# A decode kernel whose TensorE loop takes in its last round, and whose engines first visit the end of their programs

## The chip, the cores and the metric

The kernel runs on one core of one Trainium2 chip. The time is the device time in microseconds (us) of that core, and the value quoted is the median of several executions. The profile is of one execution: of the kernel before it is one more (664.23 us). Its span, from the first to the last instruction of the program, is 1.7 to 1.9 us shorter than the device time. The engines are TensorE (PE), VectorE (DVE), ScalarE (ACT), GpSimd (POOL) and SyncE (SP), which here only issues DMA transfers: all loads but that of x, and the output. SPq, PEq and DVEq are the parts of SyncE, TensorE and VectorE that issue (sequencers). PEld is TensorE loading weights.

## The reference, cut to what matters

One token passes through an attention block (32 query heads, 8 key/value heads, a cache of 65,536 positions of 128 numbers in bf16) and through a gated MLP (512 to 1,792 to 512), each with a layer norm and a residual sum.

```python
q = (layernorm(x) @ wq)                              # 512 -> 32 heads of 128
scores = einsum("bhqd,bhkd->bhqk", q, k) * 128**-0.5 # 4 query heads share one K head
o = einsum("bhqk,bhkd->bhqd", softmax(scores), v)
h = x + o @ wo
n = layernorm(h)
out = h + (sigmoid(n @ w_gate) * (n @ w_up)) @ w_down
```

The two caches are 8 x 65,536 x 128 x 2 bytes = 134 MB each. The weights add about 14 MB.

## The kernel before

The kernel loads each head's K and V in four blocks of 4 MB (so 32 K blocks and 32 V blocks, K0 to K31 and V0 to V31) into a ring of four slots. VectorE transposes a K block, TensorE forms its scores, the softmax of a head follows its fourth block, and the products with V follow one head later. Near the end the kernel loads wo, the last V blocks, then w_gate, w_up and w_down.

The kernel records all operations first and then writes them out for each engine. TensorE's operations of rounds 0 to 7 (one round for each head) form one loop. The parts A0 to A3 are the scores of a K block, the parts B0 to B3 the products of the V block of the head before, which round 0 skips. The ninth round (only B parts, for head 7, with the output projection in between) is written out after the loop:

```python
P.rounds = {"pe": (0, HKV), "dve": (1, HKV)}
...
with eng.Fori(lo, hi) as i:
    for p in order:                       # A0 B0 A1 B1 A2 B2 A3 B3
        with ExitStack() as cond:
            if lo not in parts[e][p]:
                cond.enter_context(eng.If_ne(i.val[eng.engine], lo))
            for o, w in zip(parts[e][p][hi - 1], plan[p]):
                put(e, eng, o, w)
...
for o in tail:                            # round 8, projection, MLP
    put(e, eng, o, waits_of(e, o, seen, off, False))
```

The loads are issued by SyncE in a fixed order. Each waits until the load that had its slot four loads ago has been used:

```python
order = [("wq", 0)]
order += [("K", b) for b in range(NR)]
for b in range(NR, NB):
    order += [("K", b), ("V", b - NR)]
order += [("V", NB - 4), ("V", NB - 3), ("V", NB - 2), ("V", NB - 1), ("wg", 0), ("wu", 0), ("wd", 0)]
for i, ld in enumerate(order):
    slot_of[ld] = i % NSLOT
    prev[ld] = order[i - NSLOT] if i >= NSLOT else None
```

## Time and profile before

| what | value |
|---|---|
| time, median of 3 (later of 4) runs | 664.56 us (664.51) |
| bytes moved by DMA | 282.33 MB |
| DMA busy, mean of 16 engines | 99.3% of the span |
| TensorE busy, VectorE busy | 64%, 53% |
| last piece of w_down landed | 659.50 us after the start of the span |
| end of the span | 662.6 us |

These are lines of the profile page of the kernel before: the busy time of TensorE and the other engines; the busy tenths of the DMA engines and what they moved, in 40 equal slices; the DMA queues with packets, megabytes and share; and the chain that ended last, by engine.

```profile
PE 424.0 (64%) x2385; PEld 80.5 (12%) x1617; DVE 350.6 (53%) x443; ACT 38.1 (6%) x106; POOL 5.4 (1%) x12
...
DMA  9999999999999999999999999999999999999997
GB/s 380 439 420 435 437 423 437 433 423 441 429 425 441 425 431 439 423 436 433 425 437 433 425 439 431 425 437 431 427 439 425 433 435 425 437 433 410 426 427 292
...
q1 hardware_dynamic: 11560, 282.33, 99.3%
q8 instruction: 4, 0.07, 0.0%
q14 instruction: 2, 0.02, 0.0%
...
DMA 71%; DVE 22%; PE 6%; issue 1%; SPq 0%; ACT 0%
```

DMA is at 9 tenths in 39 of 40 slices, no compute engine is near that, and the chain of waits is 71% DMA. The kernel is a stream of loads, and all else fits beside it. Two lines deserve a look: those of the queues that the page calls "instruction". I read their packets as the engines' own programs on their way in, and call them fetches; the run of GpSimd with a long program bears that out, where 2,048 more instructions bring sixteen packets of 8 KB. They move little (six packets, 80 KB), but each lasts 0.31 to 1.08 us, and the landing marks below show what that does to the stream.

The start and the end of the timeline before (start, duration, engine, source line, operation, destination and source, count; in brackets the idle time before it and what ended it):

```profile
0.74 0.40 SPq L293 DMA_DIRECT2D ring<-in_A_wq_dram  x1
...
2.39 0.29 PE L375 MATMUL PS<-ident,x_row 1*128 1x1 bf16 x4 [2.39 <-DMA x_row<-in_A_x_dram]
...
13.17 9.74 PE L394 MATMUL PS<-ring,xz 128*8 128x512 bf16 x32 [7.44 <-DMA ring<-in_A_wq_dram]
```

```profile
630.20 0.33 SPq L297 DMA_DIRECT2D ring<-in_B_w_up_dram  x1
...
652.27 1.20 PE L640 MATMUL PS<-identf,hT 128*1 128x32 f32 x32
...
655.17 0.93 PE L632 MATMUL PS<-ring,hc 128*1 128x448 bf16 x16 [1.70 <-DMA ring<-in_B_w_up_dram]
...
658.91 1.02 PE L656 MATMUL PS<-ring,hhT 128*1 128x128 bf16 x28 [0.20 <-DMA ring<-in_B_w_down_dram]
...
659.98 0.29 DVE L660 CAST y_sb<-PS 128x128 bf16<-128x128 f32 x1 [2.24 <-PE PS L656]
660.30 0.66 SPq L661 DMA_DIRECT2D out_dram<-y_sb  x1
```

The end of the chain of waits before (start, duration, what):

```profile
640.55 18.31 DMA ring<-in_B_w_down_dram
...
658.91 1.05 PE PS L656 x25
...
659.98 0.29 DVE y_sb L660
```

The first product with wq starts at 13.17 us, when wq has landed. In the tail, the products with w_up start at 655.17, when w_up has landed, and the last ones with w_down at 658.91. From there only 3.7 us are left. (The trace counts each f32 matmul of L640 twice: its 32 are 16 in the program.)

**Landing marks.** One more reading is needed, and no view of the page gives it. The trace keeps 16 landing marks for every block, as many as the page counts DMA engines, and I read each mark as one engine that is done with its share. It fits this reading that after the first fetch just one of the 16 marks of K2 is late: it is 1.56 us behind the median, the next one 0.36. So for each transfer I can read when the median engine and the last engine were done. I call the difference the lag. The packet records of the trace, which give start, duration, size and queue of each DMA packet, show when the fetches ran. For the kernel before, in us from the start of the span:

```text
instruction packets inside the span: 16 KB at 36.6, 57.0, 623.3, 649.9 (1.02 to 1.08 us each)
                                      8 KB at 54.7, 297.6 (0.31 to 0.33 us each)
transfer          median engine   last engine   lag
K1                    32.10          32.46      0.36
K2                    41.82          43.38      1.56    (fetch at 36.6 lies before this)
K31                  585.80         587.36      1.56
w_down, piece 3      657.86         659.50      1.64
```

### The profile page before, as it was taken

How to read it: one execution, taken by the hardware profiler on the slowest of the kernel's cores; microseconds unless marked ns; L12 is line 12 of the kernel's file. 1: busy time of each engine (PE TensorE's matmuls, PEld its weight loads, DVE VectorE, ACT ScalarE, POOL GpSimd, SP SyncE). 2: the span in 40 equal slices, each digit the busy share in tenths (PEclk: the TensorE clock that was granted, in tenths of full speed). 3: DMA queues.
4: the chain of work that ended last, by engine and by line, in shares of the span. 5: the costliest groups of instructions: out<-in, count | busy, mean ns of one | idle time of the engine just before them, and what ended most of it. 6: DMA issues, size and time to landing. Idle time of an engine off the chain costs nothing.

```text
span 662.6 us, 4910 instructions
## 1 busy us (share of the span) xinstructions
PE 424.0 (64%) x2385; PEld 80.5 (12%) x1617; DVE 350.6 (53%) x443; ACT 38.1 (6%) x106; POOL 5.4 (1%) x12
## 2 busy tenths in 40 slices
PE   2787487548676575576665576765856667556744
PEld 1100010011010110011100111001100111001222
DVE  3598855556337654347555463466643565553002
ACT  0200200020000200020000200002000200002000
POOL 2000000000000000000000000000000000000000
PEclk9799687678877677776866688766878867766877
DMA  9999999999999999999999999999999999999997
GB/s 380 439 420 435 437 423 437 433 423 441 429 425 441 425 431 439 423 436 433 425 437 433 425 439 431 425 437 431 427 439 425 433 435 425 437 433 410 426 427 292
DMA packets 11568, 282.42 MB, mean 426 GB/s; under 512 B 1193, under 2 KB 2218, under 8 KB 2602
## 3 DMA queue, kind: packets, MB, share of 16 engines
q1 hardware_dynamic: 11560, 282.33, 99.3%
q8 instruction: 4, 0.07, 0.0%
q14 instruction: 2, 0.02, 0.0%
q10 hardware_dynamic: 2, 0.00, 0.0%
HBM read 282.33 MB, written 0.00 MB: 426 GB/s over the span
## 4 chain that ended last, share of the span: by engine, by line
DMA 71%; DVE 22%; PE 6%; issue 1%; SPq 0%; ACT 0%
DMA ring<-in_A_k_cache_dram 62%; DVE ktw L439 20%; DMA ring<-in_A_v_cache_dram 4%; DMA ring<-in_B_w_down_dram 3%; PE PS L452 2%; DMA ring<-in_A_wq_dram 2%; PE PS L394 1%; PE PS L529 1%; DVE M_sb L444 1%; PE PS L451 1%; SPq L313 0%; DVE PT_sb L501 0%; PE PS L656 0%; PE PS L478 0%; PE PS L485 0%
## 5 line engine op out<-in xcount | busy, mean ns | idle before, releaser
L439 DVE STREAM_TRANSPOSE ktw<-ring 128x1024 f32<-128x1024 f32 x256 | 291.8, 1207 | 166.3 <-DMA ring<-in_A_k_cache_dram 165.3
L452 PE MATMUL PS<-ktw 128*128 128x512 bf16 x768 | 271.4, 452 | 54.2 <-DVE ktw L439 54.2
L451 PE MATMUL PS<-ktw 128*128 128x512 bf16 x256 | 119.0, 465 | 116.7 <-DVE ktw L439 114.9
L529 PE MATMUL PS<-ring,PT_sb 128*16 128x512 bf16 x1024 | 75.1, 444 | 12.8 <-DMA ring<-in_A_v_cache_dram 11.6
L451 PEld LDWEIGHTS PS<-ktw 128*128 128x128 bf16 x256 | 27.7, 108 | 432.8 <-issue 274.4
L501 DVE STREAM_TRANSPOSE PT_sb<-P_sb 128x512 bf16<-128x512 bf16 x32 | 20.2, 684 | 37.4 <-PE PS L539 36.0
L529 PEld LDWEIGHTS PS<-ring,PT_sb 128*16 128x16 bf16 x1024 | 30.6, 116 | 56.5 <-issue 30.0
L444 DVE TENSOR_REDUCE M_sb<-PS 128x1 f32<-128x512 f32 x32 | 19.9, 684 | 25.6 <-PE PS L451 25.6
L487 ACT ACTIVATE negmax<-PS 128x1 f32<-128x1 f32 x8 | 1.4, 171 | 545.8 <-PE PS L485 545.8
L491 ACT ACTIVATE P_sb<-PS,negmax 128x512 bf16<-128x512 f32 x32 | 21.5, 685 | 0.3
L508 DVE TENSOR_REDUCE lsum<-PS 128x1 f32<-128x4 f32 x8 | 1.3, 162 | 29.8 <-PE PS L506 29.8
L394 PE MATMUL PS<-ring,xz 128*8 128x512 bf16 x32 | 9.7, 478 | 7.4 <-DMA ring<-in_A_wq_dram 7.4
L354 DVE COPY hT<-PS 128x4 f32<-128x4 f32 x2 | 1.3, 629 | 24.9 <-PE PS L566 24.9
L478 PE MATMUL PS<-identf,gm 128*1 128x128 f32 x16 | 3.3, 292 | 17.0 <-DVE gm L476 17.0
L536 ACT ACTIVATE po_sb<-PS,rl 128x512 bf16<-128x512 f32 x8 | 5.7, 708 | 39.7 <-PE PS L529 39.7
L539 PE MATMUL PS<-sel_bf,po_sb 128*128 128x4 bf16 x32 | 2.1, 169 | 8.0 <-ACT po_sb L536 8.0
L485 PE MATMUL PS<-one_f,gmrep 1*128 1x1 f32 x16 | 4.0, 317 | 5.0 <-DVE gmrep L482 5.0
L491 ACT ACTIVATION_READ_ACCUMULATOR P_sb<-PS,negmax 128x1 f32 x32 | 6.5, 203 | 0.0
L369 POOL TENSOR_TENSOR rstd<-ve,nhalf 128x1 f32<-128x1 f32 x2 | 1.1, 553 | 645.7 <-DVE ve L367 645.7
L577 PE MATMUL PS<-ktw,O 128*1 128x512 bf16 x28 | 6.2, 379 | 0.0
L394 PEld LDWEIGHTS PS<-ring,xz 128*8 128x8 bf16 x32 | 3.2, 102 | 13.5 <-issue 11.3
L480 DVE TENSOR_REDUCE gmj<-PS 1x4 f32<-1x128 f32 x8 | 2.2, 278 | 4.1 <-PE PS L478 4.1
(85 smaller groups left out, 68.8 us busy)
## 6 DMA issues: line engine op xcount, KB each, us to landing
ring<-in_A_k_cache_dram SPq DMA_DIRECT2D x32, 4096.0 KB, 29.6
ring<-in_A_v_cache_dram SPq DMA_DIRECT2D x31, 4096.0 KB, 30.4
ring<-in_A_wq_dram SPq DMA_DIRECT2D x1, 4096.0 KB, 12.3
ring<-in_A_v_cache_dram SPq DMA_DIRECT2D x1, 3072.0 KB, 32.3
ktw<-in_A_wo_dram SPq DMA_DIRECT2D x1, 2048.0 KB, 9.6
ktw<-in_A_wo_dram SPq DMA_DIRECT2D x2, 1024.0 KB, 13.0
ring<-in_B_w_gate_dram SPq DMA_DIRECT2D x1, 1792.0 KB, 35.1
ring<-in_B_w_up_dram SPq DMA_DIRECT2D x1, 1792.0 KB, 24.9
```

Source lines behind the costliest of these rows:

```text
L394: op("pe", lambda e, kt=kt, n=n, last=last: e.matmul(ps(1, 0, 512, 0, 8), lhsT=xz[:, kt * 15 + 7 - n: kt * 15 + 15 - n], rhs=wq_v[:, kt, n ...
L439: op("dve", lambda e, d=dst, sr=src: e.transpose(d, sr), deps, f"T{b}.{c}", to="T")
L444: op("dve", lambda e, u=u: e.tensor_reduce(M_sb[:, u % 4:u % 4 + 1], ps(u % NS, 0, 512), AX.X, ALU.max), [f"S{b}.{NC - NR + k}"], f"mx{u}" ...
L451: return e.matmul(out, lhsT=lhsT, rhs=rhs, start=start, stop=stop)
L452: return e.add_instruction(mybir.InstMatmult(name=nc.get_next_instruction_name(), engine=mybir.EngineType.PE, ins=[e.lower_ap(rhs), e.lowe ...
L478: op("pe", lambda e: e.matmul(ps(MISC, 0, 128, 0, 1), lhsT=gm[:, :], rhs=identf[:, :], start=True, stop=True), [f"gm{h}"], f"gmT{h}", to="Q")
L485: op("pe", lambda e: e.matmul(ps(MISC, 128, 129), lhsT=gmrep[0:1, :], rhs=one_f[0:1, 0:1], start=True, stop=True), [f"gmrep{h}"], f"neg{h}")
L491: op("act", lambda e, b=b: e.activation(P_sb[:, (b % 4) * 512:(b % 4 + 1) * 512], ps(b % NS, 0, 512), AF.Exp, bias=negmax[:, k:k + 1], sca ...
L501: op("dve", lambda e, b=b: e.transpose(PT_sb[:, (b % 4) * 512:(b % 4 + 1) * 512], P_sb[:, (b % 4) * 512:(b % 4 + 1) * 512]), [f"E{b}", f"o ...
L529: op("pe", lambda e, lhsT=lhsT, tq=tq, t0=t0, c=c: e.matmul(ps(PO, 0, 512, 32 * tq, 32 * tq + 16), lhsT=lhsT, rhs=ring[:, s * SLOT + t0 * ...
L536: op("act", lambda e: e.activation(po_sb[:, :], ps(PO, 0, 512), AF.Copy, scale=rl[:, :]), [f"PV{NR * h + NR - 1}", f"rl{h}"], f"po{h}", to ...
L577: op("pe", lambda e, r=r, src=src, n=n, end=end: e.matmul(ps(YB, 0, D, 0, 1), lhsT=src[:, r:r + 1], rhs=ktw[:, r * D:(r + 1) * D], start=( ...
```

## The change

The change is meant to make the instruction fetches fewer and earlier. TensorE's ninth round moves into the loop: B parts run in rounds 1 to 8, A parts in rounds 0 to 7, and the projection (L) and the column step (C) only in round 8. The program becomes shorter by the second copy of the B parts. TensorE, VectorE and ScalarE run a loop of two passes around their whole programs. The first pass only branches to its end and back, under a branch hint for the back edge, which is meant to have the end of the program fetched before it is needed. For the loop to fit the last round, the last V blocks alternate between two slots, and the MLP weights get the two other slots, so that they wait for nothing in the tail. Some small operations of the tail are merged.

```diff
+                        if runs == [hi - 1]:
+                            cond.enter_context(eng.If_eq(reg, hi - 1))
+                        else:
+                            if runs[0] != lo:
+                                cond.enter_context(eng.If_ne(reg, lo))
+                            if runs[-1] != hi - 1:
+                                cond.enter_context(eng.If_lt(reg, runs[-1] + 1))
 ...
+        def twice(e, eng):
+            if self.ops[e][0]["dma"]:
+                put(e, eng, self.ops[e][0], [])
+                self.ops[e] = self.ops[e][1:]
+            with self.nc.Fori(0, 2, engines=OrderedEngineSet([eng.engine]), hint_back_edge=True) as z:
+                with eng.If_ne(z.val[eng.engine], 0):
+                    run(e, eng)
 ...
-            deco(lambda eng, e=e: run(e, eng))
+            deco((lambda eng, e=e: twice(e, eng)) if e in ("pe", "dve", "act") else (lambda eng, e=e: run(e, eng)))
 ...
+            if ld[0] == "V" and ld[1] >= NB - NR:
+                slot_of[ld] = slot_of["V", ld[1] - 2]
+                prev[ld] = ("V", ld[1] - 2)
+            elif ld[0][0] == "w" and i:
+                slot_of[ld] = 3 if ld[0] == "wd" else 1
+                prev[ld] = ("K", NB - 1 if ld[0] == "wd" else NB - 2)
 ...
-        P.rounds = {"pe": (0, HKV), "dve": (1, HKV)}
+        P.rounds = {"pe": (0, HKV + 1), "dve": (1, HKV)}
+        P.order = {"pe": ["A0", "B0", "L", "A1", "B1", "A2", "B2", "A3", "X", "C", "B3"],
+                   "dve": ["A0", "B0", "A1", "A2", "A3", "A4"]}
 ... (w_up in two pieces; 16 residual matmuls replaced by one of a spread copy of h; x added on VectorE)
```

More of the change, by code (lines that the diff above doesn't have):

```diff
@@ L4 @@
 from concourse import mybir
+from concourse.ordered_engine_set import OrderedEngineSet
 bf16 = mybir.dt.bfloat16
@@ L44, in __init__ @@
         self.rounds = {}
+        self.order = {}
         self.part = {}
@@ L143, in run @@
                     seq.append(o["part"])
-            order = [p for p, r in seq if r == hi - 1]
+            order = self.order[e]
             assert seq == [(p, r) for r in range(lo, hi) for p in order if r in parts[e][p]]
@@ L147, in run @@
                 s2 = {}
-                w = [waits_of(e, o, s2, off, True) for o in parts[e][p][r]]
+                w = [waits_of(e, o, s2, off, len(parts[e][p]) > 1) for o in parts[e][p][r]]
                 assert plan.setdefault(p, w) == w, (p, r)
@@ L155, in run @@
                         off[k] = off.get(k, 0) + n
-            regs = {}
             with eng.Fori(lo, hi) as i:
                 for p in order:
+                    runs = sorted(parts[e][p])
+                    reg = i.val[eng.engine]
                     with ExitStack() as cond:
-                        if lo not in parts[e][p]:
-                            cond.enter_context(eng.If_ne(i.val[eng.engine], lo))
-                        for o, w in zip(parts[e][p][hi - 1], plan[p]):
+                        if runs == [hi - 1]:
+                            cond.enter_context(eng.If_eq(reg, hi - 1))
+                        else:
+                            assert runs == list(range(runs[0], runs[-1] + 1)) and runs[0] - lo < 2
+                            if runs[0] != lo:
+                                cond.enter_context(eng.If_ne(reg, lo))
+                            if runs[-1] != hi - 1:
+                                cond.enter_context(eng.If_lt(reg, runs[-1] + 1))
+                        for o, w in zip(parts[e][p][runs[-1]], plan[p]):
                             put(e, eng, o, w)
@@ L204, in bass_sequential_preLN__gqa_block_cached__glu_gated_glu__decode_kernel @@
         yr = sb("yr", [1, 512], fp32)
+        gsel = sb("gsel", [128, 128], fp32)
+        hz = sb("hz", [128, 128], fp32)
         scr = sb("scr", [1, 64], fp32)
@@ L275, in bass_sequential_preLN__gqa_block_cached__glu_gated_glu__decode_kernel @@
         for i, ld in enumerate(order):
-            slot_of[ld] = i % NSLOT
-            prev[ld] = order[i - NSLOT] if i >= NSLOT else None
+            if ld[0] == "V" and ld[1] >= NB - NR:
[4 more added lines that the diff above has]
+                prev[ld] = ("K", NB - 1 if ld[0] == "wd" else NB - 2)
+            else:
+                slot_of[ld] = i % NSLOT
+                prev[ld] = order[i - NSLOT] if i >= NSLOT else None
         def freed(ld):
@@ L286, in bass_sequential_preLN__gqa_block_cached__glu_gated_glu__decode_kernel @@
         V_SPLIT = [(0, 6), (6, 8)]
+        W_SPLIT = {"wg": [(0, 4)], "wu": [(0, 3), (3, 4)]}
+        W_AT = {"wg": 0, "wu": 4 * FF}
         for ld in order:
@@ L296, in bass_sequential_preLN__gqa_block_cached__glu_gated_glu__decode_kernel @@
                 w = B_w_gate if k == "wg" else B_w_up
-                dma("sp", lambda e, d=dst, w=w: e.dma_start(d[:, 0:4 * FF].rearrange("p (k n) -> p k n", k=4),
-                    w.rearrange("(p k) n -> p k n", p=128)), f"r{s}", deps, k)
+                dst, src = dst[:, W_AT[k]:W_AT[k] + 4 * FF], w.rearrange("(p k) n -> p (k n)", p=128)
+                for i, (k0, k1) in enumerate(W_SPLIT[k]):
+                    dma("sp", lambda e, d=dst, w=src, a=k0 * FF, z=k1 * FF: e.dma_start(d[:, a:z], w[:, a:z]),
+                        f"{k}{i}", deps if i == 0 else (), f"{k}.{i}")
             elif k == "wd":
@@ L310, in bass_sequential_preLN__gqa_block_cached__glu_gated_glu__decode_kernel @@
                         dma("sp", lambda e, d=dst, sr=src, a=c0 * CH, z=c1 * CH: e.dma_start(d[:, a:z], sr[:, a:z]),
-                            f"vl{i}", deps if i == 0 else (), f"V{b}.{i}")
+                            "v0" if i else "vl", deps if i == 0 else (), f"V{b}.{i}")
                 else:
-                    dma("sp", lambda e, d=dst, sr=src: e.dma_start(d, sr), f"v{s}" if k == "V" and b < NB - NR else f"k{s}" if k == "K" and b >= NR else f"r{s}",
+                    dma("sp", lambda e, d=dst, sr=src: e.dma_start(d, sr), f"v{s}" if k == "V" else f"k{s}" if k == "K" and b >= NR else f"r{s}",
                         deps, f"{k}{b}")
@@ L348, in bass_sequential_preLN__gqa_block_cached__glu_gated_glu__decode_kernel @@
         op("dve", lambda e: e.tensor_copy(sel_bf[:, :], sel_f[:, :]), ["self"], "sel")
+        op("dve", lambda e: e.memset(gsel[:, :], 0.0), (), "gs0")
+        op("dve", lambda e: e.tensor_reduce(bass.AP(tensor=gsel, offset=0, ap=[[128, 128], [32, 4]]),
+                                            identf[:, :].rearrange("p (s j) -> p s j", s=4), AX.X, ALU.add), ["gs0", "identf"], "gsel")
         def ln_stats(i, src_dep, bank, c0):
@@ L378, in bass_sequential_preLN__gqa_block_cached__glu_gated_glu__decode_kernel @@
         op("pe", lambda e: e.matmul(ps(PO, 0, 512), lhsT=zrow[0:1, 0:128], rhs=zrow[0:1, :], start=True, stop=True),
-           ["zrow", "identf", "lsel", "onef", "sel"])
-        op("pe", lambda e: e.matmul(ps(5, 0, 128), lhsT=zrow[0:1, 0:128], rhs=zrow[0:1, 0:128], start=True, stop=True))
+           ["zrow", "identf", "lsel", "onef", "sel", "gsel"])
         ln_stats(0, ("xTp", (MISC, 0, 4)), 0, 0)
@@ L506, in denominators @@
             op("pe", lambda e: e.matmul(ps(MISC, 132, 136), lhsT=lsel[:, :], rhs=L_sb[:, :], start=True, stop=True),
-               [f"PT{NB - 1}"] if h == HKV - 1 else (), f"l{h}", to="Q")
+               [f"PT{NR * h + NR - 1}"], f"l{h}", to="Q")
             op("dve", lambda e: e.tensor_reduce(lsum[:, :], ps(MISC, 132, 136), AX.X, ALU.add), [f"l{h}"], f"ls{h}", to="D")
@@ L517, in pv @@
                     deps = []
-                    if b == NB - 1:
-                        for i, (c0, c1) in enumerate(V_SPLIT):
-                            if c == c0 and tq == 0:
-                                deps.append(f"V{b}.{i}")
-                    elif c == 0 and tq == 0:
-                        deps.append(f"V{b}")
+                    if tq == 0 and c == (V_SPLIT[1][0] if r == NR - 1 else 0):
+                        deps.append(f"V{b}" if b < NB - 1 else f"V{b}.1")
                     if c == 0 and tq == 0:
@@ L579, in project7 @@
                     skip_group_check=True), deps, "yr" if end else None)
-            op("dve", lambda e: e.tensor_copy(yr[:, :], ps(YB, 0, D, 0, 1)), ["yr"], "yrs")
+            op("dve", lambda e: e.tensor_tensor(yr[:, :], ps(YB, 0, D, 0, 1), x_row[:, :], ALU.add), ["yr"], "yrs")
         def columns():
@@ L587, in columns @@
                                                               stop=False, skip_group_check=True), ["yrs"] if nt == 0 else ())
-            op("pe", lambda e: e.matmul(ps(YT, 0, 4), lhsT=ident[:, :], rhs=xT[:, :], start=False, stop=False,
-                                        skip_group_check=True), ["xT"], "yx")
-        P.rounds = {"pe": (0, HKV), "dve": (1, HKV)}
+        P.rounds = {"pe": (0, HKV + 1), "dve": (1, HKV)}
+        P.order = {"pe": ["A0", "B0", "L", "A1", "B1", "A2", "B2", "A3", "X", "C", "B3"],
+                   "dve": ["A0", "B0", "A1", "A2", "A3", "A4"]}
         P.loop_sems = {"T": ("pe", "A3", NR * NC), "g": ("pe", "A3", 2), "W": ("pe", "A3", 1), "PT": ("pe", "B3", 1),
@@ L596, in bass_sequential_preLN__gqa_block_cached__glu_gated_glu__decode_kernel @@
         for i in range(HKV + 1):
+            loop = 0 < i < HKV
             for r in range(NR):
-                b, v = NR * i + r, NR * (i - 1) + r
-                P.part = {"pe": (f"A{r}", i), "dve": (f"A{r}", i) if i else None} if i < HKV else {}
+                P.part = {"pe": (f"A{r}", i), "dve": (f"A{r}", i) if loop else None}
                 if i < HKV:
-                    dve_block(b)
-                    pe_scores(b)
+                    dve_block(NR * i + r)
+                    pe_scores(NR * i + r)
                     if r == NR - 1:
                         softmax(i)
-                P.part = {"pe": (f"B{r}", i), "dve": (f"B{r}", i)} if i < HKV else {}
                 if i:
+                    v = NR * (i - 1) + r
+                    if r == NR - 1 and i < HKV:
+                        P.part = {"pe": ("X", i)}
+                        op("pe", lambda e: None, [f"V{v}"])
+                    elif r == NR - 1:
+                        P.part = {"pe": ("C", i)}
+                        columns()
+                        op("pe", lambda e: None, [f"V{v}.0"])
+                    P.part = {"pe": (f"B{r}", i), "dve": (f"B{r}", i) if loop else None}
                     if r == 0:
@@ L612, in bass_sequential_preLN__gqa_block_cached__glu_gated_glu__decode_kernel @@
                     if v == NB - 4:
+                        P.part = {"pe": ("L", i)}
                         project7()
-                    if v == NB - 2:
-                        columns()
-            P.part = {"dve": ("A4", i) if i else None}
+            P.part = {"dve": ("A4", i) if loop else None}
             if i < HKV:
@@ L625, in bass_sequential_preLN__gqa_block_cached__glu_gated_glu__decode_kernel @@
                                                    op0=ALU.mult, op1=ALU.add), ["tot.1"], "hc")
+        op("dve", lambda e: e.tensor_tensor(hz[:, :].rearrange("p (j k) -> p j k", k=4),
+                                            bass.AP(tensor=sel_f, offset=0, ap=[[32, 128], [1, 32], [0, 4]]),
+                                            bass.AP(tensor=hT[1], offset=0, ap=[[4, 128], [0, 32], [1, 4]]), ALU.mult),
+           ["hT.1", "self"], "hz")
         ln_rstd(1, STB, 0, 4.0)
@@ L628, in bass_sequential_preLN__gqa_block_cached__glu_gated_glu__decode_kernel @@
         for i, (nm, bank) in enumerate((("wg", GB), ("wu", UB))):
-            wv = slot_ap(slot_of[(nm, 0)])[:, 0:4 * FF].rearrange("p (k n) -> p k n", k=4)
+            at = slot_of[(nm, 0)] * SLOT + W_AT[nm]
             for kt in range(4):
                 for c in range(4):
-                    op("pe", lambda e, wv=wv, kt=kt, c=c, bank=bank: e.matmul(
-                        ps(bank, 0, FG, 32 * c, 32 * c + 1), lhsT=hc[:, kt:kt + 1], rhs=wv[:, kt, c * FG:(c + 1) * FG],
+                    dep = [f"{nm}.{j}" for j, (k0, _) in enumerate(W_SPLIT[nm]) if k0 == kt and c == 0]
+                    op("pe", lambda e, at=at, kt=kt, c=c, bank=bank: e.matmul(
+                        ps(bank, 0, FG, 32 * c, 32 * c + 1), lhsT=hc[:, kt:kt + 1],
+                        rhs=ring[:, at + kt * FF + c * FG: at + kt * FF + (c + 1) * FG],
                         start=(kt == 0), stop=(kt == 3), tile_position=(0, 32 * c)),
-                       ["hc", nm] if kt == 0 and c == 0 else (), f"gu{i}" if kt == 3 and c == 3 else None)
+                       ["hc"] * (kt == 0 and c == 0) + dep, f"gu{i}" if kt == 3 and c == 3 else None)
             if i == 0:
-                for g in range(4):
-                    for kt in range(4):
-                        dst = psap(YB, kt, [[4, 32]], 32 * g, 1)
-                        op("pe", lambda e, g=g, kt=kt, dst=dst: e.matmul(
-                            dst, lhsT=hT[1][:, kt:kt + 1], rhs=identf[:, 32 * g:32 * g + 32],
-                            start=(kt == 0), stop=False, tile_position=(0, 32 * g), skip_group_check=True),
-                           ["hT.1"] if g == 0 and kt == 0 else ())
+                op("pe", lambda e: e.matmul(ps(YB, 0, 128), lhsT=gsel[:, :], rhs=hz[:, :], start=True, stop=False, skip_group_check=True),
+                   ["hz"])
         op("act", lambda e: e.activation(sg[:, :], ps(GB, 0, FG), AF.Tanh, scale=rstd[1][:, 0:1]), ["gu0", "rstd.1"], "sg")
```

## The prediction

> **What bounds the kernel now.** The DMA stream. In the page's slices DMA is at 9 tenths in 39 of 40; its queue part gives 282.33 MB on one queue, 99.3% of 16 engines. The chain of waits is 71% DMA and ends in w_down landing at 658.87 us, then TensorE (1.05), the VectorE copy (0.29), the output DMA, end 662.6. TensorE is busy 64%, VectorE 53%. By the SyncE timeline, cache blocks are issued about 30 us before they land: nothing starves the queue. In the tail (timeline) TensorE is done with w_gate at 652.5 and waits for w_up until 655.17: 2.6 us to spare.
>
> **A small loss that the change aims at.** [...] its packet records have 16 KB instruction packets (TensorE's, I take it) at 36.6, 57.0, 623.3 and 649.9 us, about 1.04 us each, and 8 KB ones at 54.7 and 297.6. Each holds one DMA engine. In the 16 landing marks of each transfer the last engine is 0.36 us behind the median at 32 us, 1.56 at 43 (after the first fetch), and 1.64 at the last w_down piece (median 657.86, last 659.50). So fetches cost about 1.3 us at the end, as the largest lag of any engine, not as a sum.
>
> **What the change does.**
> - TensorE's last round goes into the loop: 631 matmuls in the program become 481, with weight loads about 1,255 instructions become 945: one block fewer.
> - TensorE, VectorE, ScalarE jump to the end first: last blocks are fetched[...] not at 297, 623, 650. This delays their start[...], hidden: the query matmul waits for wq until 13.17, its input is ready at 7.5.
> - About ten more branches per TensorE round: hidden; skipping a part in round 0 before shows no gap at 36.7.
> - The last V blocks share two slots; the MLP weights get slots freed by K30 and K31. V31 would be issued when V29's products end (630.2), 6.4 us before V30 lands (636.6): no starvation. Bytes and order stay.
> - 16 residual products become one (about 1 us of TensorE near 653, where it waits for DMA anyway), x is added on VectorE, w_up comes in two pieces: its last product starts 0.6 us earlier, then waits for w_down all the same.
>
> **On the critical path**: only the lag of the slowest DMA engine. I expect the fetches at 297, 623 and 650 us to go. But near 37 us TensorE still runs towards a middle block that the jump does not touch, so one fetch probably stays and leaves one engine 1.5 us behind to the end: gain about 0.2 us. If that one goes too, the gain is 1.2; if two fetches at the start meet on one engine, a loss of about 1.
>
> **Predicted**: 664.1 us, range 662.9 to 665.3. Faster by over 2%: 0.01; within: 0.98; slower: 0.01.
>
> **What would show it.** No instruction packets between 60 us and the end. V blocks still landing 9.7 us apart. Median engine's last landing near 657.9; last engine 1.2 to 1.6 behind. Chain still ends w_down, TensorE, copy, output.
>
> **What would make it wrong.** The two-slot ring starving the queue (a gap before V30 or V31, several us)[...]; the middle block fetched at the start too (663.2).

A "block" of a program is what one instruction packet carries. Its sum starts from the 664.56 us of the kernel before and has one term on the critical path, the lag: 0.2 us less (1.2 less if the fetch near 37 us goes too, about 1 more if two fetches meet on one engine). It came to 664.1 us; that is 0.26 below 664.56 - 0.2, and the text does not itemise the rest. The "one block fewer": the run with no jump shows it, with three 16 KB packets in place of four.

## The result and the profile after

| | before | after |
|---|---|---|
| median of 4 runs | 664.51 us (664.40 to 664.81) | 664.69 us (664.43 to 664.86) |
| ratio, 95% interval | | 1.0002 (0.9984 to 1.0019) |

The ratio is the mean time of the changed kernel's runs over that of the kernel before in the same rounds, so it is not quite the ratio of the medians. The time is the same; even the sign of the difference is open.

The same lines of the page after:

```profile
PE 426.3 (64%) x2353; PEld 79.6 (12%) x1585; DVE 351.1 (53%) x446; ACT 38.6 (6%) x106; POOL 5.4 (1%) x12
...
DMA  9999999999999999999999999999999999999996
GB/s 379 439 425 429 439 425 433 439 419 439 439 417 437 441 419 437 433 427 437 433 427 437 431 427 439 425 433 439 423 433 441 419 435 439 421 437 404 436 421 285
...
q1 hardware_dynamic: 11704, 282.33, 99.3%
q8 instruction: 3, 0.05, 0.0%
...
q14 instruction: 1, 0.00, 0.0%
...
DMA 66%; DVE 22%; PE 10%; issue 1%; SPq 0%; ACT 0%; DVEq 0%
```

The stream looks the same. The 16 KB instruction packets (queue q8) are three in place of four; of the 8 KB ones (q14) the line still lists one small packet, and the packet records show no 8 KB one before the end of the span. The same places of the timeline and of the chain:

```profile
0.74 0.39 SPq L322 DMA_DIRECT2D ring<-in_A_wq_dram  x1
...
8.44 0.26 PE L409 MATMUL PS<-ident,x_row 1*128 1x1 bf16 x4 [8.44 <-issue]
...
14.55 9.72 PE L427 MATMUL PS<-ring,xz 128*8 128x512 bf16 x32 [4.62 <-DMA ring<-in_A_wq_dram]
```

```profile
630.71 0.80 SPq L341 DMA_DIRECT2D ring<-in_A_v_cache_dram  x2
...
653.35 0.80 PE L678 MATMUL PS<-hz,gsel 128*128 128x128 f32 x2
...
659.17 1.01 PE L692 MATMUL PS<-ring,hhT 128*1 128x128 bf16 x28 [0.55 <-DMA ring<-in_B_w_down_dram]
...
660.23 0.29 DVE L696 CAST y_sb<-PS 128x128 bf16<-128x128 f32 x1 [2.62 <-PE PS L692]
660.55 0.65 SPq L697 DMA_DIRECT2D out_dram<-y_sb  x1
```

```profile
633.46 25.66 DMA ring<-in_B_w_down_dram
...
659.17 1.04 PE PS L692 x23
660.23 0.29 DVE y_sb L696
```

TensorE begins at 8.44 us, not at 2.39: its trip to the end of the program cost 6 us. It did not matter, because the products with wq waited for wq anyway. But they start at 14.55 us, not 13.17, and that is because wq itself lands later (14.41 us, against 13.03 before). The landing marks show why:

```text
after: instruction packets of 16 KB inside the span at 5.3, 36.9, 47.6; of 8 KB: none
transfer          median engine   last engine   lag    next two engines
wq                    12.71          14.41      1.71   0.36, 0.17
K2                    41.83          43.71      1.88   1.73, 0.17
K3                    51.53          53.44      1.90   1.73, 1.70
w_down, piece 3      658.07          659.75      1.69   1.52, 1.51
```

Each fetch beside the stream puts one DMA engine 1.7 to 1.9 us behind the median one, and that engine stays behind for the remaining 600 us. (The marks don't name their engine; that it is the same one is read from lags that hardly change from one block to the next.) Three fetches lie on three engines here. TensorE goes on only when the last engine has landed: the last products with w_down start at 659.17 us, after the last engine's 659.12 for the second piece, not after the median's 657.43. So the end of the stream is where it was: the lag was 1.71 us after the one fetch at 5.3 us and is 1.69 at the end, after three; before the change it was 1.64, after four and with one of them as late as 650 us.

The packet records show what a lag is made of. The fetch at 36.93 us lasts 1.05 us. The stream's next packet of 32 KB starts as it ends and takes 1.68 us, where 1.21 to 1.23 is usual. The 1.05 and the 0.47 on top make 1.5 us. Between 12 and 600 us just two of the 7,755 stream packets of that size are longer than 1.23 us, and both follow an instruction packet; before the change four are, and so do they.

One thing stays unexplained: from wo on, a fourth engine is 1.5 us behind, with no instruction packet near. It doesn't set the end, since others are further behind. V blocks still land 9.7 us apart (V29 to V30: 627.22 to 636.93), so the two slots of the tail do not starve the queue.

### The profile page after: what moved, and what is told of

It reads as the page before. It is cut to its first block, busy times and chain, and to the rows that moved or that the text cites. A ratio compares the mean times of both kernels' runs of the same rounds, so it can differ in the third digit from the quotient of the medians.

```text
span 663.0 us, 4962 instructions
## 1 busy us (share of the span) xinstructions
PE 426.3 (64%) x2353; PEld 79.6 (12%) x1585; DVE 351.1 (53%) x446; ACT 38.6 (6%) x106; POOL 5.4 (1%) x12
## 4 chain that ended last, share of the span: by engine, by line
DMA 66%; DVE 22%; PE 10%; issue 1%; SPq 0%; ACT 0%; DVEq 0%
DMA ring<-in_A_k_cache_dram 57%; DVE ktw L472 20%; PE PS L485 4%; DMA ring<-in_B_w_down_dram 4%; DMA ring<-in_A_v_cache_dram 3%; DMA ring<-in_A_wq_dram 2%; PE PS L558 2%; PE PS L484 2%; PE PS L427 1%; DVE M_sb L477 1%; DVE PT_sb L534 1%; PE PS L518 0%; PE PS L511 0%; SPq L328 0%; PE PS L692 0%
## 5 line engine op out<-in xcount | busy, mean ns | idle before, releaser
L558 PE MATMUL PS<-ring,PT_sb 128*16 128x512 bf16 x1024 | 78.4, 459 | 16.7 <-DMA ring<-in_A_v_cache_dram 10.7
## 6 DMA issues: line engine op xcount, KB each, us to landing
ring<-in_A_k_cache_dram SPq DMA_DIRECT2D x32, 4096.0 KB, 29.6
ring<-in_A_v_cache_dram SPq DMA_DIRECT2D x31, 4096.0 KB, 29.6
```

The source lines that it names most:

```text
L558: op("pe", lambda e, lhsT=lhsT, tq=tq, t0=t0, c=c: e.matmul(ps(PO, 0, 512, 32 * tq, 32 * tq + 16), lhsT=lhsT, rhs=ring[:, s * SLOT + t0 * ...
```

## The experiments

The theory, called "lag" below: the stream ends with the DMA engine that instruction fetches have put furthest behind; lags on different engines do not add up, lags on one engine do. Two rivals: "compensation", that the jump gains about 1 us and the rest of the change gives it back; and "bandwidth", that fetches have nothing to do with the end. All kernels gave correct results. The first four ran beside the kernel before (664.53 us, 7 runs, 664.35 to 665.13), the last two on another chip (664.51 us, 7 runs, 664.38 to 664.96).

The table counts from the issue of the first load, since two kernels delay it on purpose. It is of the profiled run of each kernel.

| kernel | 16 KB instruction packets, us | first load issued | median engine's last landing, after the first load | last engine's | lag |
|---|---|---|---|---|---|
| before | 36.6, 57.0, 623.3, 649.9 | 0.74 | 657.12 | 658.76 | 1.64 |
| after | 5.3, 36.9, 47.6 | 0.74 | 657.33 | 659.01 | 1.69 |
| no jump | 36.4, 46.4, 654.9 | 0.74 | 657.17 | 658.92 | 1.76 |
| jump only | 5.1, 37.5, 57.2, 621.3, 648.0 | 0.74 | 657.47 | 660.56 | 3.09 |
| late loads | 2.1, 40.5, 51.0 | 5.60 | 657.20 | 658.95 | 1.75 |
| tour | 2.6, 5.7, 9.0 | 9.23 | 657.15 | 657.45 | 0.30 |
| tour beside the loads | 6.4, 12.7, 19.7 | 0.74 | 657.24 | 659.14 | 1.91 |

The median engine ends within 0.35 us of the same moment in all seven. What differs is the lag.

### No jump

```diff
-            deco((lambda eng, e=e: twice(e, eng)) if e in ("pe", "dve", "act") else (lambda eng, e=e: run(e, eng)))
+            deco(lambda eng, e=e: run(e, eng))
```

> The changed kernel without the jump to the end (loop of nine rounds, slots and tail as changed). Theory lag (the end is set by the DMA engine that an instruction fetch has put furthest behind; lags on different engines do not add): within 0.3 us of 664.5; 16 KB instruction packets near 37 and 47 us and one more near 650 us in place of the one at 5.3 us; 8 KB ones back near 55 and 298 us; the last engine still 1.4 to 1.8 us behind the median at the last landing. Rival compensation (the jump gains about 1 us and the rest of the change gives it back): about 665.7 us. Rival bandwidth (fetches do not matter for the end): 664.5 us.

Measured: 664.80 us (664.58 to 665.84), ratio to before 1.0008 (0.9992 to 1.0025). The packets came as expected: 16 KB at 36.4, 46.4 and 654.9 us, 8 KB at 54.9 and 297.4. The lag at the end is 1.76. So the jump moves one TensorE fetch from 655 to 5 us and takes the two 8 KB fetches out of the stream, and the time is the same with it or without it. The rival compensation asked for 665.7 us as the usual time; only one of four runs was that long.

### Jump only

```diff
 # in the kernel before; loop, slots and tail as they were
+        def twice(e, eng):
+            ... (as in the change)
-            deco(lambda eng, e=e: run(e, eng))
+            deco((lambda eng, e=e: twice(e, eng)) if e in ("pe", "dve", "act") else (lambda eng, e=e: run(e, eng)))
```

> The kernel before with the jump alone, loop and tail as before. Theory lag: within 0.3 us of 664.5; one of the two 16 KB packets at 623 and 650 us gone, one near 5 us new, those near 37 and 57 us stay; 8 KB ones at 55 and 298 us gone; last engine 1.4 to 1.9 us behind the median. Rival compensation: about 663.4 us. Rival bandwidth: 664.5 us.

Measured: 665.12 us (664.75, 664.75, 665.50, 666.66), ratio 1.0007 (0.9990 to 1.0023). Compensation, with 663.4 us, falls: the jump alone gains nothing. I had expected one of the two late fetches to go; both stayed, at 621.3 and 648.0 us, so without the shorter program the jump adds a fetch and saves no TensorE fetch inside the span. The queue line of the page shows six 16 KB packets; the sixth, at 663.1 us, comes after the output was issued and is left out of the table:

```profile
q8 instruction: 6, 0.10, 0.1%
```

The profiled run was the longest one, 666.66 us, and shows an accident that supports the theory. The fetch at 648.0 us fell on an engine that was already 1.60 us behind:

```text
jump only             median   last    lag    next two engines
V31, second part      645.24  646.84   1.60   1.34, 1.24
w_gate                649.53  652.66   3.13   1.34, 1.24
w_down, piece 3       658.21  661.30   3.09   1.27, 1.21
```

Two fetches on one engine add up, and this run is 2.1 us longer than the median of the kernel before, although the median engine is only 0.35 us later. Only this one run's records show such a meeting. That the other long runs of these kernels (665.84 us with no jump, 665.50 here) have the same cause is a guess.

### Late loads

```diff
                 with eng.If_ne(z.val[eng.engine], 0):
+                    if e == "pe":
+                        eng.sem_inc(self.toured, 1)
                     run(e, eng)
 ...
+                if e == "sp":
+                    eng.wait_ge(self.toured, 1)
```

> The changed kernel, but SyncE's first load waits until TensorE is back from its jump, so that this one fetch is over before the stream starts. The first load starts d us later[...]. Theory lag: the fetches near 37 and 47 us (plus d) remain, the last engine stays 1.4 to 1.9 us behind, time 664.6 + d. Rival bandwidth: the same. It measures d and what one fetch costs without the stream beside it; it is the control of the next run.

Measured: 669.25 us (668.93 to 669.55). The first load was issued at 5.60 us, so d is 4.86. 664.6 + 4.86 = 669.5, against 669.55 in the profiled run; both the theory and the bandwidth rival say so, and the run is the control of the next one. The fetch at 2.1 us, now before the stream, leaves no mark: wq, K0 and K1 land with a lag of 0.30. After the fetch at 40.5 us the lag is 1.80, and a second engine is 1.41 us behind after the one at 51.0. So here the fetch ahead of the stream left no engine behind, and each of those beside it did.

### Tour

TensorE runs one empty round ahead of the nine. Head and tail of its program are inside the loop too, each under its branch, so the empty round branches through the whole program. TensorE's jump of the change is taken out. SyncE's first load waits for the empty round.

```diff
-            with eng.Fori(lo, hi) as i:
+            with eng.Fori(lo, hi + dry) as i:               # dry = 1 for TensorE
+                if dry:
+                    with eng.If_eq(i.val[eng.engine], 1):
+                        eng.sem_inc(self.toured, 1)
+                        for o, w in heads:
+                            put(e, eng, o, w)
                 for p in order:
+                            if dry:
+                                cond.enter_context(eng.If_ne(reg, 0))
 ... (all other conditions one round later; the tail under If_eq on the last round; SyncE waits as in late loads)
```

> The changed kernel, but TensorE first runs an empty round through its whole program (every part skipped by its branch), so that all blocks are fetched, and SyncE's first load waits for it. The first load starts D us later[...]. Theory lag: no 16 KB instruction packet after the first load, the last engine at most 0.5 us behind the median at all landings, and the time is 664.6 + D - 1.3, counted from the first load issue 1.3 us shorter than the kernel before. Rival bandwidth: counted from the first load issue as long as the kernel before (within 0.3 us).

Measured: 672.12 us (671.72 to 672.43), and the profiled run, 671.72. These are lines of the profile of the tour: its DMA queues, SyncE's first load, and the end of the chain of waits.

```profile
q1 hardware_dynamic: 11704, 282.33, 98.2%
q8 instruction: 3, 0.05, 0.0%
```

```profile
9.23 0.39 SPq L341 DMA_DIRECT2D ring<-in_A_wq_dram  x1
```

```profile
639.37 27.31 DMA ring<-in_B_w_down_dram
...
666.73 0.41 PE PS L711 x8
667.16 0.29 DVE y_sb L715
```

Three 16 KB packets are fetched as in the changed kernel, but all begin before the first load is issued, at 2.6, 5.7 and 9.0 us. D is 9.23 - 0.74 = 8.49 us. In the stream no engine falls behind any more: the lag is 0.24 at wq, at most 0.35 in the tail, and 0.30 at the last piece; none of the 32 KB packets between 16 and 600 us takes longer than 1.23 us. Counted from the first load, the stream ends at 657.45 us in place of 658.76: 1.31 us earlier, the 1.3 that the theory asked for and the bandwidth rival excluded. From the profiled run's time, 671.72 - 8.49 = 663.23 us, against 664.53 before. (The median of the four runs gives 663.63, if D was the same in all, which only the profiled run shows.) So the loss is real and this is its size, but the remedy costs far more: the packets come 3.0 and 3.3 us apart, one after the other, although no load has been issued yet.

### GpSimd with a long program

```diff
+        gum = sb("gum", [1, 2048], mybir.dt.uint8)
 ...
+        for i in range(2048):
+            op("pool", lambda e, i=i: e.memset(gum[:, i:i + 1], 0))     # after the first rstd
```

> The changed kernel, but GpSimd, which idles through the stream, runs 2,048 one-byte memsets on bytes that nobody reads after its first small operation. Its program grows by 128 KB, which has to be fetched beside the stream (16 packets of 8 KB or 8 of 16 KB). Theory lag: each fetch puts one engine 0.5 to 1.4 us further behind; packets that hit the same engine add up, so the last engine ends 2.3 to 4 us behind the earliest and the time is 0.6 to 2.5 us longer than the changed kernel's 664.7. Rival bandwidth: 128 KB more at 426 GB/s over all engines is 0.3 us, so at most 665.0 us.

(What the kernel before shows of fetches lies within the 0.5 to 1.4 us: the 8 KB one at 297.6 us left a mark 0.68 us behind the median, the 16 KB one at 36.6 us raised the lag by 1.2, from 0.36 to 1.56.)

Measured: 673.15 us (673.01 to 673.47), ratio to before 1.0129 (1.0113 to 1.0146). That is 8.6 us longer than the kernel before, far above both expectations. Sixteen 8 KB packets appear, 128 KB for the 2,048 memsets, so one for each 128 of them, with one every 5.5 us from 18 to 101 us. They all fall on one engine; the lag grows by some 0.65 us with each:

```text
GpSimd long           median   last    lag     next engine
K0                     22.39   23.99   1.60    0.49
K2                     41.80   44.93   3.13    1.66
K4                     61.24   66.99   5.76    1.65
V2                    109.79  120.15  10.36    1.66
V28                   605.25  615.54  10.29    1.72
wo, first piece       619.11  620.44   1.33    0.27
w_down, piece 3       666.87  668.15   1.28    0.32
```

At K0 the last engine is one that served a TensorE fetch, and GpSimd's is the next one; from K1 on GpSimd's is the last. The packet records account for it: each of the sixteen lasts 0.31 us, and the stream packet right behind it takes 1.57 us in place of 1.21 (the first 1.46): 0.31 and 0.35 on top make 0.66. The memsets themselves, which all write to one partition, could have been a rival; but apart from the two behind TensorE's fetches no other stream packet of 32 KB from 15 to 120 us is longer than 1.23 us.

GpSimd pays too. It stands idle for 1.2 to 1.4 us before each fetched block of 128 memsets, 18.7 us in all, waiting for nothing that the profile shows:

```profile
L419 POOL MEMSET gum<- 1x1 uint8 x2048 | 69.7, 97 | 18.7 <-issue 18.7
```

Of this kernel, the slices of the page, the queue of the 8 KB packets, and SyncE's issue of wo:

```profile
GB/s 374 437 433 431 429 423 430 437 433 433 431 424 433 435 433 431 428 428 437 433 433 433 426 430 435 433 435 428 426 435 433 433 435 428 428 435 205 437 413 294
...
q14 instruction: 16, 0.13, 0.0%
```

```profile
611.72 1.28 SPq L355 DMA_DIRECT2D ktw<-in_A_wo_dram  x3
```

For 500 us an engine that is 10 us behind costs nothing, since the loads are issued three blocks ahead (in the changed kernel a block lands 29.6 us after its issue, one every 9.7 us). The bill comes at wo, which may be loaded only when the scores of K31 are done: K31 lands whole at 596.14 us, not 587.68, so wo is issued at 611.72, not 602.91. The 15 other engines had finished V28 by 607 (half of them by 605.3) and stood idle; that is the slice with 205 GB/s. While they wait, the late engine catches up: the lag falls from 10.29 to 1.33, and the median engine is from there on 9 us later than in the changed kernel (619.11 against 610.15). Neither expectation had foreseen that one engine takes all the fetches of GpSimd, nor that the loss would come at wo and not at the end, where the lag is only 1.28. The bandwidth rival (at most 665.0) falls. The theory's rule, that lags on one engine add, holds; its size was wrong by more than a factor of three, because I had spread the fetches over several engines.

### Tour beside the loads

```diff
 # the tour, without SyncE's wait
-                if e == "sp":
-                    eng.wait_ge(self.toured, 1)
```

> The empty first round of TensorE as in the run with the tour, but the loads start at once, as before the change. Theory lag: the three 16 KB fetches now lie in the first 20 us, none after, but beside the stream; the engines that served them stay 1.4 to 1.8 us behind to the end (3 if two meet on one engine), so the time is within 0.4 us of 664.6. If only the moment of the fetches mattered (early is free): 663.3 us.

Measured: 664.77 us (664.56 to 665.09), ratio 1.0002 (0.9986 to 1.0019). All three fetches lie in the first 20 us, 6.3 to 7.0 us apart, and none after. Only TensorE's program differs from the changed kernel here, so the three 16 KB packets are TensorE's. Three engines are 1.85, 1.57 and 1.56 us behind at K1; at the end the largest lag is 1.91. TensorE starts at 16.25 us (its first matmul in the timeline), after wq has landed (14.75). That is hidden as well: K3, the first load that waits for the products with wq, is issued 4 us later than in the changed kernel (28.29 against 24.30) and lands at the same time (53.45 against 53.44).

```profile
16.25 0.26 PE L426 MATMUL PS<-ident,x_row 1*128 1x1 bf16 x4 [16.25 <-issue]
```

So early fetches were not free here. Only those ahead of the first load left no lag (0.30 us at the end of the tour), and in the tour they delayed the first load by 8.49 us. No kernel tried here beats the kernel before.

## Why the prediction was right

- **The bound** was right: the median DMA engine ends 657.12 to 657.47 us after the first load in all kernels of the table, whatever happens to TensorE.
- **The landings**: the median engine's last one came at 658.07 us (657.9 predicted), the last engine 1.69 us later, just above the 1.2 to 1.6 that I had given.
- **The fetches at 297, 623 and 650 us go**: right; after 60 us no instruction packet is left inside the span, so nothing of TensorE's loop was fetched again in the rounds that follow. In the run with no jump it shows who did what: the shorter program takes one TensorE fetch away, the jump moves one from 655 to 5 us and takes the two 8 KB ones out of the stream. The prediction gives all three to the jump; jump only shows that by itself it takes neither of TensorE's late ones away.
- **The gain is the change of the largest lag, not a sum**: right, and it carried the prediction. Three fetches fewer beside the stream (two of 8 KB, one of 16 KB) changed the lag from 1.64 to 1.69 us. I had put the gain at 0.2 us (and the time at 664.1, which is 0.46 below where the kernel stood); the medians differ by +0.18 us, within the runs' scatter, so not even the sign is shown.
- **One fetch stays near 37 us**: it did, but a second stayed too, at 47.6 us. It made no difference, because the three are on three engines.
- **If the middle one goes too, 1.2 us**: wrong as it stood, and luck that it didn't matter. The prediction counted fetches moved to the start as free. The one at 5.3 us alone left an engine 1.71 us behind, so the gain would have failed even without those at 37 and 47.6 us. The case that it put at 663.2, all of TensorE's blocks fetched at the start, is the tour beside the loads: 664.77. The size was right: the tour shows 1.31 us, once no fetch is beside the stream. The predicted range, 662.9 to 665.3, holds both outcomes, so the time alone could not tell them apart.
- **Two fetches on one engine cost about 1 us**: the long run of jump only shows it, with a lag of 3.09 in place of 1.64, so nearer 1.5.
- **The delayed start is hidden**: right. TensorE lost 6 us (8.44 against 2.39), with its fetch at 5.3 us, beside the first loads (in late loads the fetch is at 2.1, ahead of them, and TensorE starts at 5.78).
- **Branches, slots, merged tail**: hidden, as predicted. TensorE shows no idle time at the fetch of 36.9 us, and near 47.6 us only waits of 0.5 to 0.75 us for VectorE. The first product with w_down starts at 657.70 us, against 657.80. V30 and V31 land without a gap, and TensorE still waits for w_down at the end.

What stays open: which DMA engine serves a fetch. GpSimd's sixteen all went to one, TensorE's three or four mostly to different ones, and in one run two met. Nothing here shows what decides it. Nor do the records show where the two 8 KB blocks came from in the kernels with the jump; no such packet appears in their spans, although the branch was taken.

## What to carry to other kernels

In a kernel that is one long DMA stream, read the landing of the last DMA engine apart from the median one: a single interruption of one engine stayed to the end here, and removing some of the interruptions gained nothing until none was left (lag at the end 1.64 us before, 1.69 after, 0.30 in the tour). Before you shorten or prefetch a program for the sake of its fetches, compare the whole possible gain (here 1.3 us of 664) with the cost of a fetch outside the stream (in the tour some 3 us for each 16 KB packet). And look for the points where the queue runs dry, since in the GpSimd run that is where a late engine's lag was paid by all.
